# Linear attention in blocks of 64 tokens on 64x64 tiles of TensorE, and x with its tokens on partitions

## The chip, the cores and the metric

The kernel runs on one core of a Trainium2 chip. The metric is device time in microseconds (us) for one execution of the whole kernel, as the median of several executions. A matrix engine (TensorE, PE in the profile), a vector engine (VectorE, DVE), a scalar engine (ScalarE, ACT) and GpSimd (POOL) work side by side, each through its own instructions in order; SyncE (SP) issues most of the transfers. Matmul results land in eight banks of 128 partitions x 512 float32 each (PSUM), which GpSimd does not read here; everything else is in the on-chip memory SBUF.

## What is computed

Decayed linear attention over 4 batches, 8 heads, 768 tokens and a head dimension of 64, then a token mixer of rank 32, then a two-layer MLP of 512 to 2048 to 512, all in float32. Cut to what matters:

```
for b in range(nb):                      # blocks of 64 tokens, per batch and head
    intra = ((qb @ kb.T) * Dmask) @ vb   # Dmask[i, j] = lam**(i-j), lower triangle
    inter = (qb * lam**(i+1)) @ kv_state
    x[:, block] = intra + inter
    kv_state = lam**64 * kv_state + (kb * lam**(63-i)).T @ vb
u  = x + mixed                           # mixed = low-rank map over the 768 tokens
out = u + relu(u @ w_ch1) @ w_ch2
```

The block size is a matter of how the recurrence is cut, not of the result: any block size gives the same x.

## The kernel before

The work has three stages. The **front** makes x from q, k and v, mixes it over tokens, turns it and splits it for the products. The **first product** multiplies the turned u by w_ch1 (`hidden`, L624). The **second product** multiplies by w_ch2 (`product`, L760). Both products hold each float32 operand as a high and a low part, three matmuls for one.

The change lies in the front. It runs in 24 steps, one for each tile of 128 tokens of a batch (`NS` is 24, `NT`, the tiles of a batch, is 6). The instructions of every engine are issued in an order written out by hand: the list `pieces` (L494 to L508) names the pieces of each step, and L598 runs them. Side work that converts U, V and the first columns of w_ch1 from 64-bit words is dealt to the steps by `aside`.

A step s of the kernel before works on one block of 128 tokens. `prep` (L299) turns q and k of step s+1 by eight transposes on TensorE; ScalarE copies them to `qt` and `kt` (L310). `scale` (L326) lets GpSimd multiply q by powers of lam (`qs`) and k by decays (`ks`). `scores` (L334) makes k times q for each head into two banks `pss`, with keys on partitions, one head on rows 0 to 63 of the array and the other on rows 64 to 127; VectorE multiplies by the mask into `sm` (L347, two instructions). `outputs` (L350) adds the state's part (L359) and the scores' part (L364) in `px`, which has head dimensions on partitions, and ScalarE copies it to `xt` (L369). `state` (L373) makes the block's own k times v in `pkv` (L380); VectorE adds it to the faded state `kvc` (L389, four instructions), and ScalarE copies that into the block-diagonal `kv` (L395, two instructions). `back` (L399) turns `xt` so that tokens are on partitions (L404, four transposes), and ScalarE copies the result to `x_nat` (L406).

From step 7 on, three more pieces run on an earlier tile: `mix` (L444) adds the mixed part to x (one matmul, one VectorE add), `turn` (L455) turns u by four transposes and VectorE makes high and low parts (L469, L480), and the closure `rest` (L482), run as `turned` one step later, makes two ScalarE copies and one GpSimd subtraction (L486). When a batch's six tiles are complete (steps 6, 12 and 18), `low` and `low_sum` (L411, L431) compute its rank-32 part.

All PSUM tiles come from one pool with two buffers for each of the four tags a1, a2, b1 and b2. The first product starts while the last pieces of the front are still open: `rest` (L691) places them between its matmuls.

```
step += [("mix", done)] * (done >= 0)
step += [("outputs", s)]
step += [("scores", s + 1), ("back", s)] * (s + 1 < NS)
step += [("turn", done)] * (done >= 0 and done // TG < FG)
```

## Time and profile before

| what | value |
| --- | --- |
| median of 8 runs | 699.95 us (698.78 to 700.42) |
| profiled execution, its own time | 698.78 us |
| span of the profiled execution | 697.0 us |
| front, start to the first matmul of the first product | 141.6 us |
| first product | 141.6 to 420.9 us |
| second product | 420.9 to 697.0 us |
| TensorE busy in the front | 136.8 of 141.6 us |
| VectorE, ScalarE, GpSimd busy in the front | 104.6, 101.3, 66.9 us |
| busy share of the transfer engines, 0 to 50.7 and 50.7 to 141.6 us | 0.90 and 0.63 |
| granted TensorE clock | 1.00 throughout |

How to read it: the profile gives each engine's busy time, the duration of each group of instructions by source line and shape, the chain of work that ended last (followed back from the last instruction), and for every wait of an engine what ended it. A float32 matmul that is not a transpose shows as two records on PE and two weight loads on PEld; a transpose shows as one. Matmuls overlap in the pipeline, so the time from one start to the next tells more than a duration: a record of pkv lasts 222 ns, yet sixteen of them take 0.5 us. The profiled execution was the fastest of the eight; 1.8 us of its time lie around the span.

### The profile page before, as it was taken

To read this page: it belongs to the slowest core of one execution; us is meant where nothing else is said; L and a number is where in the kernel's file an instruction comes from. 1 tells how busy PE (TensorE), PEld (TensorE's weight loads), DVE (VectorE), ACT (ScalarE), POOL (GpSimd) and SP (SyncE) were. 2 spreads that over 40 slices of the span, in tenths; PEclk is the share of its full clock that TensorE was granted. 3 is DMA by queue.
4 is the path that set the end of the run, shared out by engine and by line. 5 is a ranking of instruction groups with operands and counts; after the bars stand their busy time and mean duration, and the time that the engine had idled before them with its cause. 6 is when DMAs were issued, how large, how long until landed. Compare 5 with 4: busy or idle time off the path is not lost.

```text
span 697.0 us, 11418 instructions
## 1 busy us (share of the span) xinstructions
PE 685.5 (98%) x4194; PEld 555.5 (80%) x4194; DVE 502.2 (72%) x905; ACT 306.5 (44%) x543; POOL 108.1 (16%) x91
## 2 busy tenths in 40 slices
PE   8999999998999999999999999999999999999997
PEld 6979787876888888888888888888888888888886
DVE  5778687867899777777779435777687586775864
ACT  4867777844566544444455322232232222322320
POOL 4425555523000000000000000011030030300300
PEclk9999999999999999999999999999999999999999
DMA  9977686224476565656557889966344363353531
GB/s 212 226 192 184 175 215 165 83 90 162 171 260 240 204 211 208 208 209 207 203 207 261 293 315 354 342 204 200 99 156 149 91 211 101 124 184 91 166 92 60
DMA packets 131530, 131.17 MB, mean 188 GB/s; under 512 B 81234, under 2 KB 89426, under 8 KB 131474
## 3 DMA queue, kind: packets, MB, share of 16 engines
q1 hardware_dynamic: 129376, 129.92, 59.0%
q10 hardware_dynamic: 2098, 0.52, 0.3%
q8 instruction: 33, 0.54, 0.3%
q14 instruction: 23, 0.19, 0.1%
HBM read 80.09 MB, written 50.33 MB: 187 GB/s over the span
## 4 chain that ended last, share of the span: by engine, by line
PE 93%; DVE 4%; issue 1%; ACT 1%; DMA 1%; ACTq 0%; DVEq 0%
PE pz L638 25%; PE pz L771 13%; PE pz L769 13%; PE pd L773 13%; PE pd L648 13%; PE pss L341 3%; PE px L364 3%; PE px L359 2%; PE pxn L404 2%; PE pkv L380 2%; PE put L464 1%; PE pk L306 1%; PE pq L306 1%; DVE ut L469 1%; DVE sm L347 1%
## 5 line engine op out<-in xcount | busy, mean ns | idle before, releaser
L638 PE MATMUL pz<-u_hl,w 128*128 128x512 f32 x768 | 190.7, 398 | 1.1 <-ACT uf L476 1.1
L638 PEld LDWEIGHTS pz<-u_hl,w 128*128 128x128 f32 x768 | 144.4, 188 | 37.1 <-ACT uf L476 1.5
L771 PE MATMUL pz<-w_hl,m 128*128 128x512 f32 x384 | 151.6, 396 | 0.0
L769 PE MATMUL pz<-w_hl,m 128*128 128x512 f32 x384 | 151.6, 396 | 0.0
L773 PE MATMUL pd<-w_d,m 128*128 128x512 f32 x384 | 150.0, 396 | 0.0
L752 ACT ACTIVATE m<-mt 128x512 fp32r<-128x512 f32 x96 | 60.7, 632 | 196.3 <-PE pd L773 133.3
L753 DVE SCALAR_TENSOR_TENSOR m<-rm,m 128x512 fp32r<-128x512 f32 x96 | 71.5, 745 | 49.5 <-ACT m L752 49.2
L653 DVE SCALAR_TENSOR_TENSOR r<-pd,r 128x512 f32<-128x512 f32 x96 | 61.8, 686 | 57.7 <-ACT r L644 47.2
L793 POOL TENSOR_TENSOR o<-o,u 128x512 f32<-128x512 f32 x20 | 29.9, 1523 | 452.1 <-DVE o L791 452.1
L648 PE MATMUL pd<-u_d,w 128*128 128x512 f32 x384 | 98.8, 397 | 0.0
L773 PEld LDWEIGHTS pd<-w_d,m 128*128 128x128 f32 x384 | 72.3, 188 | 17.6
L769 PEld LDWEIGHTS pz<-w_hl,m 128*128 128x128 f32 x384 | 72.3, 188 | 17.6
L771 PEld LDWEIGHTS pz<-w_hl,m 128*128 128x128 f32 x384 | 72.3, 188 | 17.6
L648 PEld LDWEIGHTS pd<-u_d,w 128*128 128x128 f32 x384 | 72.2, 188 | 17.4
L644 ACT ACTIVATE r<-pz 128x512 f32<-128x512 f32 x96 | 51.9, 592 | 62.8 <-PE pz L638 62.8
L754 DVE SCALAR_TENSOR_TENSOR m<-m 128x512 fp32r<-128x512 f32 x96 | 69.1, 721 | 0.9
L751 DVE TENSOR_SCALAR mt<-rm 128x512 uint32<-128x512 uint32 x96 | 46.2, 482 | 30.0 <-DMA rm<-r_d 29.6
L347 DVE TENSOR_TENSOR sm<-pss,mask 128x512 f32<-128x512 f32 x48 | 30.9, 686 | 10.9 <-PE pss L341 8.9
L179 ACT CAST w<-wt 128x512 fp32r<-128x512 f32 x32 | 19.9, 622 | 41.8 <-DVE wt L176 33.6
L364 PE MATMUL px<-sm,vraw 128*64 128x128 f32 x384 | 35.8, 274 | 0.4 <-DVE x_nat L450 0.3
L359 PE MATMUL px<-qs,kv 128*64 128x128 f32 x320 | 32.1, 279 | 0.0
L136 ACT ACTIVATE sc<-sc,ends 128x512 f32<-128x512 uint32 x29 | 21.0, 723 | 19.2 <-DVE sc L132 19.2
(88 smaller groups left out, 761.3 us busy)
## 6 DMA issues: line engine op xcount, KB each, us to landing
r_d<-r SPq DMA_DIRECT2D x96, 256.0 KB, 2.9
rm<-r_d SPq DMA_DIRECT2D x96, 256.0 KB, 2.7
words<-in_moe_w_ch_dram SPq DMA_DIRECT2D x32, 512.0 KB, 4.6
w_d<-w SPq DMA_DIRECT2D x16, 768.0 KB, 3.3
w_hl<-w_d SPq DMA_DIRECT2D x16, 512.0 KB, 6.6
u_d<-x_nat SPq DMA_DIRECT2D x24, 256.0 KB, 3.1
u<-u_d SPq DMA_DIRECT2D x24, 256.0 KB, 4.3
out_dram<-o SPq DMA_DIRECT2D x24, 256.0 KB, 2.0
```

What stands on the lines that cost most here:

```text
L364: nc.tensor.matmul(out=px[x * D : (x + 1) * D, a, :], lhsT=vr[:, 2 * a + x, :], rhs=sm[:, x, a, :], start=(c == 0), stop=True,)
L638: nc.tensor.matmul(out=acc[g][0], lhsT=w[:, n, ct, :], rhs=uhl[g][:, n, ct, :], start=(ct == 0 and n == 0), stop=(ct == CT - 1 and n == 1),)
L644: nc.scalar.mul(rs[g], acc[g][0], 1.0 + E)
L648: nc.tensor.matmul(out=acc[g][1], lhsT=w[:, 2, ct, :], rhs=ud[g][:, ct, :], start=(ct == 0), stop=(ct == CT - 1),)
L653: nc.vector.scalar_tensor_tensor(rs[g], acc[g][1], 4096.0, rs[g], ALU.mult, ALU.add)
L751: nc.vector.tensor_scalar(t.bitcast(U32), r.bitcast(U32), HI, None, ALU.bitwise_and)
L752: nc.scalar.activation(out=m[:, 0], in_=t, func=AF.Relu)
L753: nc.vector.scalar_tensor_tensor(m[:, 1], r, 0.0, hi, ALU.max, ALU.subtract)
L754: nc.vector.scalar_tensor_tensor(m[:, 2], hi, E, low, ALU.mult, ALU.subtract)
L769: nc.tensor.matmul(out=pz, lhsT=m[:, 0, cols], rhs=hl[:, 0], start=first, stop=False)
L771: nc.tensor.matmul(out=pz, lhsT=m[:, 1, cols], rhs=hl[:, 1], start=False, stop=end)
L773: nc.tensor.matmul(out=pd, lhsT=m[:, 2, cols], rhs=dd, start=first, stop=end)
```

## The change

The attention part of a step now takes its 128 tokens as two blocks of 64, and each of its matmuls takes 64 rows and 64 columns of the array, so that four of them have disjoint quarters of it.

- `ahead_of(s)` takes the place of `scores` and `state`. For each head and each block it multiplies `ks` with v (16 matmuls into half of a two-bank tile `psk`) and k with q (16 matmuls into the other half). VectorE then forms the state before the second block, `kvb` (one addition to the already faded state), the state after it, `kva` (four instructions), and the masked scores `sm` in one instruction instead of two. `sm` has two buffers.
- `fade(s)` is new: four ScalarE instructions that multiply `kva` by lam**64.
- `inter(s)` and `intra(s)` take the place of `outputs` and `back`. The sums have tokens on partitions, so `xt`, its four transposes and its copy are gone; one ScalarE copy takes `px` to `x_nat`.
- Because two row groups of the array add to the same sums, a small ScalarE copy `seen` waits for the last matmul of `inter`, and the second half of `intra` waits for `seen`.
- The block-diagonal `kv` and its two ScalarE copies are gone; masks and powers are 64 wide; `powers` runs before the first step; `ks` is made for every tile, the last of a batch included.
- In the front every PSUM tile has one buffer: `psk` and `px` take two banks each, and q, k, the turned u and the mixer's product take one each. The former pool is opened when the front's is closed.
- The order within a step is new: `scale` comes before `turned` on GpSimd, and `mix` of tile 17 moves from the first product to the end of the front. k and v get a fourth raw buffer, and more loads are issued at the start.

```
+    def fade(s):
+        if s % NT > 0:
+            st[s]["faded"] = faded = att.tile([P, HP, D], FP32, tag="faded", name="faded")
+            for a in range(HP):
+                nc.scalar.mul(faded[:, a, :], kva[s][:, a, :], lamc[:, a, :])
+
+    def ahead_of(s):
+        ks, vr, qt, kt = (st[s].pop("ks"), raw[s, "v"], st[s]["qt"], st[s]["kt"])
+        both = two_banks("psk", "sk")
+        c = s % NT
+        pss = both[:, :, 0 : HP * D].rearrange("p x (a i) -> p x a i", a=HP)
+        pkv = both[:, :, HP * D :].rearrange("p t (a e) -> p t a e", a=HP)
+        blocks = range(2 if c < NT - 1 else 1)
+        for a in range(HP):
+            for x in range(2):
+                for t in blocks:
+                    nc.tensor.matmul(
+                        out=pkv[half[x], t, a, :], lhsT=ks[half[t], a, x, :],
+                        rhs=vr[half[t], 2 * a + x, :], start=True, stop=True,
+                    )
+        for a in range(HP):
+            for t in range(2):
+                for x in range(2):
+                    nc.tensor.matmul(
+                        out=pss[half[t], x, a, :], lhsT=kt[half[x], a, half[t]],
+                        rhs=qt[half[x], a, half[t]], start=True, stop=True,
+                    )
+        kvb[s] = att.tile([P, HP, D], FP32, tag="kvb", bufs=2, name="kvb")
+        if c == 0:
+            nc.vector.tensor_copy(out=kvb[s], in_=pkv[:, 0])
+        else:
+            nc.vector.tensor_tensor(
+                out=kvb[s], in0=pkv[:, 0], in1=st[s].pop("faded"), op=ALU.add
+            )
+        if c < NT - 1:
+            kva[s + 1] = att.tile([P, HP, D], FP32, tag="kva", bufs=2, name="kva")
+            for a in range(HP):
+                nc.vector.scalar_tensor_tensor(
+                    kva[s + 1][:, a, :], kvb[s][:, a, :], lamc[:, a, :], pkv[:, 1, a, :],
+                    ALU.mult, ALU.add,
+                )
+        sm = att.tile([P, 2, HP, D], FP32, tag="sm", bufs=2, name="sm")
+        nc.vector.tensor_tensor(out=sm, in0=pss, in1=mask, op=ALU.mult)
+
+    def inter(s):
+        c = s % NT
+        st[s]["px"] = both = two_banks("px", "px")
+        px = both[:, :, 0 : HP * D].rearrange("p x (a e) -> p x a e", a=HP)
+        for a in range(HP):
+            for x in range(2):
+                for t, kv in enumerate((kva, kvb)):
+                    if t > 0 or c > 0:
+                        last = nc.tensor.matmul(
+                            out=px[half[t], x, a, :], lhsT=st[s]["qs"][half[x], a, t, :],
+                            rhs=kv[s][half[x], a, :], start=(a == 0), stop=False,
+                        )
+        st[s]["seen"] = nc.scalar.copy(
+            att.tile([P, 1], FP32, tag="seen", name="seen"), small[:, 4:5]
+        )
+        wait_for(st[s]["seen"], last)
+
+    def intra(s):
...
+        for i in range(2):
+            for a in range(HP):
+                for t in range(2):
+                    x = i ^ t
+                    mm = nc.tensor.matmul(
+                        out=px[half[t], x, a, :], lhsT=sm[half[t], x, a, :],
+                        rhs=vr[half[t], 2 * a + x, :],
+                        start=(c == 0 and t == 0), stop=(a == HP - 1 or (c == 0 and t == 0)),
+                    )
+                    if i == 1 and seen is not None:
+                        wait_for(mm, seen)
+                        seen = None
+        xs[s] = x_pool.tile([P, C], FP32, tag="x", name="x_nat")
+        nc.scalar.copy(xs[s].rearrange("p (a x e) -> p x a e", a=HP, x=2), px)
...
-        step = [("prep", s + 1)] * (s + 1 < NS)
-        step += [("turned", done - 1)] * (done > 0)
-        step += [("scale", s + 1)] * (s + 1 < NS)
-        step += [("aside", s)]
+        step = [("prep", s + 1), ("fade", s + 1)] * (s + 1 < NS)
         step += [("mix", done)] * (done >= 0)
         step += [("low", b - 1)] * (c == 0 and b > 0)
-        step += [("outputs", s)]
+        step += [("inter", s)]
+        step += [("scale", s + 1)] * (s + 1 < NS)
+        step += [("turned", done - 1)] * (done > 0)
+        step += [("aside", s)]
+        step += [("ahead_of", s + 1)] * (s + 1 < NS)
         step += [("low_sum", b - 1)] * (c == 0 and b > 0)
-        step += [("scores", s + 1), ("back", s)] * (s + 1 < NS)
+        step += [("intra", s)]
         step += [("turn", done)] * (done >= 0 and done // TG < FG)
         pieces += step
+    pieces += [("mix", NS - NT - 1)]
...
-        (0, 0, "mix", c0 - 1), (0, 4, "back", NS - 1), (0, 4, "enter", None),
+        (0, 4, "enter", None),
```

## The prediction

> **What bounds the kernel now.** I read the stage windows first: both products keep TensorE busy 98 to 99% and the change leaves their instructions alone, so the 141.6 us front decides. Next the chain of waits (start, length, what), here one late step of the front, from the scores of tile 16 to those of tile 17:

> ```profile
> 95.76 1.09 PE pss L341 x16
> 96.85 0.60 PE pxn L404 x4
> 97.45 0.44 PE put L464 x4
> 97.89 0.44 PE pq L306 x4
> 98.33 0.43 PE pk L306 x4
> 98.99 0.37 PE px L359 x4
> 100.89 0.55 PE pkv L380 x16
> 101.44 1.09 PE pss L341 x16
> ```

> Nothing but PE stands there; `mix` (0.24 us) lies before px at 98.99, and px runs to 100.89. Then the windows of an early step and of two late ones (bounds, length, busy PE, PEld, DVE, ACT, POOL, clock, transfer share, GB/s):

> ```profile
> 16.18:21.10 4.92, 4.92 (x79) 4.56 (x78) 3.25 (x11) 3.93 (x9) 2.34 (x2) 1.00 1.01 234
> ...
> 84.33:90.01 5.68, 5.68 (x84) 5.14 (x83) 4.63 (x10) 4.08 (x8) 3.03 (x4) 1.00 0.69 173
> ...
> 95.76:101.44 5.68, 5.68 (x83) 5.14 (x83) 4.63 (x10) 5.05 (x10) 2.44 (x3) 1.00 0.89 241
> ```

> PE fills every step; the other engines have about 1 us to spare in 5.68. So a cut on PE counts until one of them, or the transfers, binds. Steps 0 to 5 cost 4.9 us; the 15 late ones 5.7; steps 6, 12 and 18, with `low`, about 7.5.

> **TensorE, the main term.** The question is how many small matmuls run at once. One row of the groups by form (busy us, mean ns), then of PE's timeline (start, length) tell:

> ```profile
> L380 PE MATMUL pkv<-vraw,ks 128*64 128x64 f32 x49 | 2.3, 228 | 0.0
> ...
> 89.32 0.69 PE L380 MATMUL pkv<-vraw,ks 128*64 128x64 f32 x16
> 89.94 1.16 PE L341 MATMUL pss<-qt,kt 64*128 64x128 f32 x16
> ...
> 73.83 1.06 PE L415 MATMUL pp<-x_nat,u_w 128*32 128x512 f32 x8
> 74.71 0.61 PE L424 MATMUL pp<-x_nat,u_w 128*32 128x256 f32 x8
> ```

> pkv's 16 records start in pairs, one per column half, every 58 ns: 8 slots in 0.47 us. pss's start in pairs, one per row half, every 111 ns: 8 slots in 0.89, and 0.2 more of its 1.09 for the change of tiling. pp has four column quarters: 8 records take 0.88 us where one 512-wide float32 record alone takes 0.53 (pr, 1.07 for two), so four run together. The window of its start shows four records begun in 0.04 us:

> ```profile
> 73.82:73.86 0.04, 0.03 (x4) 0.03 (x5) 0.00 (x0) 1.00 0.54 205
> ```

> No row shows halves of rows and of columns at once. Its price per record of N=64 lies between 58/4 = 14.5 ns and 58 ns (no overlap). I take 14.5: halves overlap fully in either direction, quarters do in one, and records begin about 7 ns apart.

> Late step before: prep 0.87, mix 0.24, put 0.44, px 1.90, pkv 0.55, pss 1.09, pxn 0.59 = 5.68. After: prep, mix, put stay, 1.55. inter, pkv and pss have 16 matmuls each, 32 records in 8 slots of 58 ns, 0.47 each, 1.41. intra has the same 32 records, but token block and rows coincide, so only two tiles are used: 16 slots, 0.93. Changes of tiling fall from four a step to two, 0.4. Sum **4.3 us**. Early (no mix, no put): 3.6.

> [...] The rows say 128 attention records cost 2.34 us. [...]

> **VectorE.** One of two sm instructions goes (686 ns each), kvb comes (128x256, 425 ns as the copy at L387); kva's four take 0.86, as kvc's did. From 4.63 to about 4.4 busy. Laid end to end: ut 0.69, u_hl 0.62, mix 0.61, kvb 0.37, kva 0.86, sm 0.65, side work 0.6 on average, 0.2 of semaphores: **4.6**. This is the next bound.

> **ScalarE.** Gone: xt 0.58 and two kv copies of 0.405. New: four fades and `seen`. No row has an ACT instruction of 64 columns; the copies of 512 (587 ns) and 256 columns (372) put one at about 0.21, and a scaled one, as te's 631, at 0.26. Between 0.15 (overlapped) and 0.35 each; I take 0.22, 0.9 together, and 0.2 for `seen`. From a mean of 4.57 over three late steps to 4.3.

> **The added wait.** `seen` waits on ACT for inter's last matmul; behind it are u_hl's and te's copies, side casts and the copy to x_nat, and POOL's subtraction waits for te. intra's second half waits for `seen`; behind it on PE are turn and the next prep. Walk from prep's start: q is turned after 0.69 (pq at 97.89 in the chain, as ACT starts qt), qt 0.48, kt 0.6, fades 0.9, `seen` 0.3, second half of intra 0.47, put with its change 0.6: 4.05 round the loop. It is shorter than VectorE's 4.6, which hides it; uncovered, a late fade costs PE its own length. psk's single tile is free once sm has read it, some 2 us of VectorE before it is needed; px's when x_nat is copied, before inter.

> **GpSimd and queues.** qs 1.28, ks 1.06, the subtraction 1.28: 3.6 of 4.6, and with scale first qs no longer queues behind te. The extra ks (four in all) hide there. SP issues the same loads, v after intra, u's store after turn; ks(s+2) needs k two steps ahead, which the fourth buffers serve. Transfers: q, k, v are 0.786 MB a step, 3.4 us at 234 GB/s, and the early window is at share 1.01. Early steps can hardly go below 3.6; I charge **1.5 us** for the lag. Late ones need 4.2 us of transfer time (3.4, and u's 0.25 MB at some 0.35 MB/us) below 4.7.

> **Ends.** v and ks now stand before the first scores: v's load, issued at 2.29, lands after 5.5 (its row), 7.8; pss ended at 8.34 and will at about 8.8: 0.5 lost, halved masks and early `powers` fit before it. At the other end pxn (0.44) leaves the first product, but mix of tile 17 is followed by VectorE's addition (0.68 and 0.25 to be seen) before pz may reuse the bank: 0.5 lost net.

> **Sum.** Late cadence 4.7 (VectorE's 4.6, 0.1 of hand-over) for 5.68: 0.98 x 15 = 14.7. Early 3.9 for 4.9: 1.0 x 6 = 6.0. Steps with `low` lose VectorE's and ACT's slack: 0.8 x 3 = 2.4. Less 1.5, 0.5, 0.5: **20.6 us**. The profiled execution's own time is 698.8 (the lowest of eight, median 699.95, so the median may come out a microsecond higher): **678 us**.

> **Rivals.**
> - [...] 0.13.
> - *Hand-overs*: VectorE, ACT and PE all near 4.5, single PSUM buffers and `seen` make each wait for the slowest of the step, cadence 5.3 and early 4.5: 0.38 x 15 + 0.4 x 6 + 1 = 9, **689**. For: side work is uneven, 1.4 us of ACT in some steps (L136, L137). Against: two steps' slack on sm. 0.15.
> - *Tiles pair at most two at a time*, 29 ns a record: 1.95 + 3.7 = 5.65, **697 to 699**, no change. 0.05.
> - *Slower*: row and column halves don't overlap in this form, so that weight load and matmul of one tile hold the next. Place: the 128 attention records; it decides above (5.68 - 1.95) / 128 = 29 ns a record, which is pkv's present pace. At 40 ns a step is 7.1, 24 x 1.4 = 34 more, **733**. For: PEld is busy 5.14 of 5.68. Against: both directions overlap singly. 0.07.
> - That the four-wide work doesn't happen is covered by the last two.

> My case has 0.60. Its own best end is cadence 4.4 and early 3.6 (PE's), 28 to 30 us, 668. Up to the two rivals at 688 and 689 with 3 us of spread: **667 to 692**, leaving 0.12 out. A measurement tells some 0.2% (1.4 us) from no change: faster 0.88, within 0.05, slower 0.07.

> **What would show it.** Late steps (pss to pss) of 4.6 to 4.8 us with VectorE at 4.4 busy and PE idle some 0.4; inter, pkv and pss each in 0.5 to 0.65 us, intra in about 1; PE waiting for VectorE more than for ACT; the first product's first matmul near 121 us and the stages behind it as long as before. I am wrong if the 64x64 groups take 0.9 us or more, if fades exceed 0.35 us each, if PE's waits are on transfers, or if the products lengthen.

## The result, and the profile after

The changed kernel takes **695.3 us** as a median of 11 runs (692.77 to 698.51), against 699.52 us for the kernel before in the same comparisons (31 runs, 698.62 to 701.09): a ratio of 0.994, with a 95% interval from 0.9929 to 0.9952. It is faster, by some 4 us, where the prediction's sum had 20.6; 678.0 is missed by 17.3 us and the range's upper end by 3.3. The profiled execution's own time is 693.19 us around a span of 691.4.

The first product starts at 136.35 us instead of 141.61 and everything behind it is as long as before (555 us), so the whole difference lies in the front, and so does the whole miss: the forecast had about 121.

First what went as forecast. The chain of waits of the kernel after, over one late step (start, length, what):

```profile
50.16 0.62 PE px L417 x32
50.78 0.47 PE psk L379 x32
51.25 0.47 PE psk L386 x32
51.72 0.93 PE px L435 x32
52.65 0.59 PE put L504 x4
53.24 0.44 PE pq L329 x4
53.67 0.44 PE pk L329 x4
54.11 0.23 PE pu L487
54.34 0.62 PE px L417 x32
```

The step takes 4.18 us where the old one took 5.68. Thirty-two records of the state products take 0.47 us, of the scores 0.47, of `intra` 0.93, of `inter` 0.47 and the change of tiling. Four 64x64 tiles do run at once: four records of `inter` start between 50.55 and 50.57 us, and each lasts 0.22. Now windows of the kernel after: two stretches of the front, and two whole steps, one undisturbed and one near the end (bounds, length, busy PE, PEld, DVE, ACT, POOL, clock, transfer share, GB/s):

```profile
16.00:49.00 33.00, 25.92 (x798) 21.61 (x790) 19.94 (x49) 19.60 (x53) 13.42 (x12) 0.95 0.88 208
...
84.00:106.00 22.00, 15.84 (x528) 14.36 (x529) 19.41 (x36) 13.61 (x35) 13.90 (x12) 1.00 0.81 208
```

```profile
58.64:63.10 4.46, 4.46 (x146) 4.11 (x147) 4.39 (x11) 3.75 (x12) 3.74 (x3) 1.00 1.00 241
119.54:124.56 5.02, 5.02 (x201) 4.71 (x205) 4.92 (x13) 4.99 (x15) 4.78 (x4) 1.00 0.46 145
```

And the same two stretches in the kernel before:

```profile
16.00:49.00 33.00, 32.02 (x459) 27.34 (x455) 23.60 (x51) 23.84 (x47) 12.71 (x11) 1.00 0.91 214
...
84.00:106.00 22.00, 22.00 (x314) 19.86 (x312) 18.01 (x41) 17.00 (x34) 12.21 (x11) 1.00 0.79 204
```

TensorE was busy 32.0 and 22.0 us in these two stretches before; now it stands for 7.1 of 33 us and for 6.2 of 22. For what does it stand? The waits of TensorE from 7 to 136 us (line, what for, us in total, times, longest):

```profile
PE px L435 <- issue: 6.6, 5, 2.0
PE pq L329 <- issue: 3.6, 2, 2.1
PE px L417 <- issue: 1.6, 3, 1.0
PE px L417 <- ACT x_nat L444: 1.4, 1, 1.4
PE psk L379 <- DMA vraw<-in_v_dram: 1.4, 1, 1.4
PE pk L329 <- DVE vp L480: 1.2, 3, 0.7
PE pk L329 <- issue: 1.0, 1, 1.0
```

12.8 of these us (6.6, 3.6, 1.6 and 1.0) are "issue": time in which the engine waited for nothing that the profile shows. TensorE has no such wait in the front of the kernel before, where all its waits from 7 us on come to 1.4 us. One of them in the chain, ahead of the transposes of q:

```profile
86.65 0.60 PE put L504 x4
87.25 2.05 issue
89.30 0.60 PE pq L329 x4
89.90 0.44 PE pk L329 x4
```

In the records of that stop the first weight load of `pq` starts at 86.97 us, so its semaphores had been passed; the matmul that belongs to it starts at 89.30. Between this weight load and its matmul stands no wait at all, as if TensorE had not yet got the next instruction. The queue of the transfers that carry instructions fits that. Here are the rows of the list of queues, first before, then after (packets, MB, share of 16 engines):

```profile
q8 instruction: 33, 0.54, 0.3%
```

```profile
q8 instruction: 44, 0.72, 0.4%
```

Eleven more packets of 16,384 bytes, all in the front: 15 before its end in the kernel before, 26 after. TensorE issues 3,755 weight loads, matmuls and semaphore instructions there before and 6,649 after, so 250 and 256 to a packet. If the stops are TensorE running out of a packet, they must lie where packets meet. Numbering its instructions from the first one and dividing by 256 gives, for the stops of over 0.35 us between 15 and 134 us (worked out from the records; the packet is the last one that started before the restart):

```
stop (us)          length  awaited by name  remainder  packet starts  to restart
 20.03 -  21.04     1.01   nothing             193         18.82         2.22
 24.17 -  25.19     1.02   nothing             194         22.97         2.22
 28.20 -  30.23     2.03   nothing             194         27.57         2.66
 35.62 -  37.16     1.53   nothing             193         34.71         2.45
 40.43 -  40.99     0.56   nothing             194         38.68         2.31
 48.57 -  49.27     0.70   vp                  246
 83.67 -  84.11     0.44   nothing             193         81.40         2.70
 87.24 -  89.30     2.06   nothing             193         86.92         2.38
 92.87 -  93.41     0.54   nothing             194         90.61         2.80
 97.90 -  99.75     1.85   nothing             194         97.47         2.27
103.73 - 105.34     1.61   nothing             194        102.88         2.46
131.45 - 132.88     1.43   x_nat               119
```

All ten stops without a named wait restart at remainder 193 or 194, the two with one do not. So these look like the packets' boundaries. The cause, as it looked before any experiment: a step of the new kernel is some 293 records in 4.46 us (the window above), a packet's worth every 3.9 us; the old one is 166 in 5.68, a packet's worth every 8.8. In this kernel no packet's first instruction ran less than 2.19 us after the packet had started, and a packet started 1.9 us after the boundary before it (a median of 25 packets). The two add to some 4.1 us for 256 instructions, an estimate of the least time between two boundaries, and the new steps use them in just about that.

### The profile page after: what moved, and what is told of

The parts are those of the page before. It is cut to its first block, busy times and chain, and to the rows that moved or that the text cites. A ratio compares the mean times of both kernels' runs of the same rounds, so it can differ in the third digit from the quotient of the medians.

```text
span 691.4 us, 14352 instructions
## 1 busy us (share of the span) xinstructions
PE 662.6 (96%) x5634; PEld 535.7 (77%) x5634; DVE 502.8 (73%) x918; ACT 297.1 (43%) x583; POOL 117.9 (17%) x98
## 4 chain that ended last, share of the span: by engine, by line
PE 90%; DVE 5%; issue 3%; ACT 1%; DMA 1%; ACTq 0%; DVEq 0%
PE pz L685 25%; PE pz L818 13%; PE pz L816 13%; PE pd L820 13%; PE pd L695 12%; PE px L435 3%; PE px L417 2%; PE psk L379 2%; PE psk L386 2%; PE put L504 1%; PE pk L329 1%; PE pq L329 1%; DVE ut L509 1%; DMA vraw<-in_v_dram 1%; PE pp L455 1%
## 5 line engine op out<-in xcount | busy, mean ns | idle before, releaser
L695 PEld LDWEIGHTS pd<-u_d,w 128*128 128x128 f32 x384 | 72.2, 188 | 17.4
L352 POOL TENSOR_TENSOR qs<-qt,powq 128x512 f32<-128x512 f32 (+1 forms) x24 | 28.4, 1185 | 44.8 <-ACT qt L333 32.9
L435 PE MATMUL px<-vraw,sm 64*64 64x64 f32 x768 | 29.1, 220 | 6.6 <-issue 6.6
L435 PEld LDWEIGHTS px<-vraw,sm 64*64 64x64 f32 x768 | 26.2, 135 | 9.5 <-issue 9.5
L136 ACT ACTIVATE sc<-sc,ends 128x512 f32<-128x512 uint32 x29 | 21.0, 723 | 19.2 <-DVE sc L132 19.2
```

Source lines behind the costliest of these rows:

```text
L435: mm = nc.tensor.matmul(out=px[half[t], x, a, :], lhsT=sm[half[t], x, a, :], rhs=vr[half[t], 2 * a + x, :], start=(c == 0 and t == 0), sto ...
L695: nc.tensor.matmul(out=acc[g][1], lhsT=w[:, 2, ct, :], rhs=ud[g][:, ct, :], start=(ct == 0), stop=(ct == CT - 1),)
```

## The experiments

Each ratio is against the kernel before on the same chip; "stops" are TensorE's waits for "issue" from 7 us to the end of the front in the profiled execution, 12.8 us in the changed kernel.

**Loads that are shorter.** The changed kernel, with the same bytes of q, k and v read as contiguous rows of 2 KB; the tokens and heads that meet are then other ones, so x is that of permuted data.

```diff
-                in_=source[b, h : h + n, c * P : (c + 1) * P, :].rearrange("h p d -> p h d"),
+                in_=source[b].rearrange("h s d -> (h s d)")[c * P * C : (c + 1) * P * C].rearrange(
+                    "(p h d) -> p h d", h=H, d=D
+                )[:, h : h + n, :],
```

> The changed kernel, but each q, k and v load takes the same 256 KB as 128 rows of 2 KB instead of 1024 rows of 256 bytes (tokens and heads arrive permuted, so x differs from the reference); instructions of the engines are unchanged. Pages theory (TensorE stops because its own instructions arrive in 16 KB pages that land late while the transfer engines are loaded): the stops with no named wait shrink from some 12 us in the front to under 5, time 684 to 690. Data theory (TensorE waits for q, k or v and the profile doesn't name it): about the same, 683 to 690. Hand-over theory (ScalarE and VectorE in order, the seen wait): within 1 us of the changed kernel's 695.

Measured: 691.9 to 693.4 us in three executions, ratio 0.9904 (0.9887 to 0.992). A gain of some 2.5 us over the changed kernel, less than either theory of transfers expected. The fourth execution, the profiled one, took 2272 us, so no line of it tells where the gain comes from. Inconclusive.

**More instructions in the old kernel.** The kernel before, with each 128-column matmul of `pss` and `px` issued as two of 64 columns.

```diff
-            for x in range(2):
-                rows = slice(x * D, (x + 1) * D)
+            for cols in (slice(0, D), slice(D, P)):
+                for x in range(2):
...
-                    out=pss[x][:, a, :], lhsT=kt[rows, a, :], rhs=qt[rows, a, :],
+                    out=pss[x][:, a, cols], lhsT=kt[rows, a, :], rhs=qt[rows, a, cols],
```

> The kernel before, with each matmul of 128 columns in px and pss issued as two of 64: the same columns streamed and the same loads, but about 260 TensorE instructions a step for 165. Pages theory: stops of 0.5 to 2 us with no named wait appear on TensorE, each within 3 us after a 16 KB instruction packet begins; time 703 to 715. Data theory and hand-over theory: data and hand-overs are as before, so within 1.5 us of 699.5.

Measured: 721.61 us, ratio 1.0319 (1.0303 to 1.0334), and not one stop. The chain of this kernel, part of a late step:

```profile
104.14 0.23 PE px L367 x8
104.37 0.47 PE pkv L383 x16
104.84 1.93 PE pss L342 x32
106.77 0.59 PE pxn L407 x4
```

32 records of `pss` take 1.93 us, as long as 32 of full width would (1.98, an estimate: twice the 0.89 and once the 0.2 for the change of tiling of the 1.09 that 16 took before). Halving the columns did not shorten `pss`, whose matmuls still load weights of 128 columns each; it did halve the records of `px`, whose weights have 64 (eight in 0.23 us, where px took 1.90 us for 32 before). So the kernel got slower by work, its 260 or so records spread over a step of some 6.6 us, and a packet lasted some 6.4 us. By the estimate of 4.1 us above no stop is due at this pace, so as an experiment on supply it fails. What it does say: 260 records a step (293 in the changed kernel) brought no stop here, at 6.6 us a step for 4.46.

**No late loads.** The changed kernel loads q, k and v for the first three tiles only and uses them again, so its x is that of three tiles' data.

```diff
+        if s >= 3:
+            raw[s, name] = kept[s % 3, name]
+            return
```

> The changed kernel with q, k and v loaded for the first three tiles only and used again by the later ones (x differs from the reference). Pages theory and data theory: the stops go, steps run at 4.3 to 4.6 us throughout and early ones below 4, the first product begins at 113 to 121 us, time 674 to 682. Theory that the dense 64x64 stream itself outruns the pages: stops of 1 to 2 us stay even with idle transfer engines, time above 688. Hand-over theory: above 690.

Measured: 682.63 us, ratio 0.9769 (0.9749 to 0.9789); the front ends at 126.05. Both are a little behind what was expected of the two transfer theories (682 at most, 121 at most). The waits of TensorE in it:

```profile
PE px L438 <- issue: 2.7, 3, 1.1
...
PE pk L332 <- issue: 0.5, 1, 0.5
```

Stops fall from 12.8 to 3.6 us with the same 44 instruction packets, and those that remain over 0.35 us without a named wait all lie at remainder 194. (One more of 0.76 us lies there too; the profile puts it down to TensorE's own `pq` before it.) A packet now starts 1.03 us after the boundary before it (median), not 1.93. Although the changed kernel waited for loaded data only once (1.4 us, at the start), taking the loads away is worth 12.7 us (12.0 by the ratios): with the loads each packet starts 0.9 us later. Not all of the gain is stops: this version's four executions were granted 0.999 to 1.000 of the clock, the changed kernel's 0.990 to 0.998, of which more at the end.

**The columns of w_ch1 fetched later.** Two fetches of words moved from steps 5 and 15 to 12 and 19.

```diff
-        (w1_steps(1), (5, 15, 16, 17, 18, 19, 20, 21)),
-        (w1_2[:3], (15, 22, 23)),
+        (w1_steps(1), (12, 15, 16, 17, 18, 19, 20, 21)),
+        (w1_2[:3], (19, 22, 23)),
```

> The changed kernel with the fetch of the second and third columns of w_ch1 moved from steps 5 and 15 to steps 12 and 19. Pages theory: less transfer load around 38 and 91 us, some of the stops go, 1 to 5 us faster than the changed kernel. Data theory: the same sign, but only if a named or unnamed wait for q, k, v is at those places. Hand-over theory: within 1 us of 695.

Measured: 696.47 us (12 runs, 692.73 to 701.07), ratio 0.9965 (0.9947 to 0.9983), stops 10.5 us. The stops moved to other boundaries (remainder 193 or 194 still). No gain, where 1 to 5 us were expected.

**Fewer instructions, the same loads.** `qt`, `kt`, `qs`, `kvb` and `kva` in bfloat16: the scores and `inter` are one pass of TensorE each, at lower precision.

```diff
-        qt, kt = (att.tile([P, HP, P], FP32, tag=n, bufs=2, name=n) for n in ("qt", "kt"))
+        qt, kt = (att.tile([P, HP, P], BF16, tag=n, bufs=2, name=n) for n in ("qt", "kt"))
```

> The changed kernel with qt, kt, qs, kvb and kva in bfloat16, so that the scores and inter are one pass each of TensorE in place of float32's passes: some 218 TensorE instructions a step in place of some 282, the same loads, stores and order; its output is of lower precision in these two products. Theory 1 (TensorE runs out of instructions while their 16,384-byte packets queue behind the loads): a packet lasts a third longer, so most stops without a named wait go (12.65 us of the front in the changed kernel, under 5 us here) and about 32 to 38 instruction packets are fetched in the whole run; TensorE's own work falls too, by up to 0.6 us a step where it binds; 680 to 687 us. Theory 2 (it is the loads of q, k and v that TensorE waits for, unseen): loads are as they were, so the stops stay near 12 us; only the cut of TensorE's work counts where no stop hides it, 690 us or more. Theory 3 (VectorE and ScalarE bind the steps): no gain, 693 to 697.

Measured: **678.41 us**, ratio 0.9703 (0.9689 to 0.9718), 38 instruction packets, the front's end at 118.96. All of theory 1's numbers came in, the time even below them. TensorE's waits from 7 to 136 us and one window, to be held against the changed kernel's above:

```profile
PE px L418 <- ACT x_nat L445: 3.6, 3, 1.6
PE psk L380 <- issue: 3.6, 6, 1.0
PE pk L330 <- DVE vp L481: 1.8, 3, 0.8
PE psk L380 <- DMA vraw<-in_v_dram: 1.4, 1, 1.4
PE psk L380 <- DVE sm L406: 1.2, 1, 1.2
```

```profile
84.00:106.00 22.00, 20.69 (x523) 16.71 (x518) 21.62 (x49) 18.08 (x47) 17.18 (x15) 1.00 0.99 252
```

Waits for "issue" are 4.0 us in all (3.6 and 0.4, one of them not among these lines), and of these only one, of 0.40 us, lies at a packet's boundary (194). The other six, 3.6 us, are at 235, 55, 20 and such, and are of another kind: each restarts 0.10 us after VectorE has ended `sm` (worked out from the records), as the one of 1.2 us does that the profile puts down to `sm`. The state products of a next tile wait there until `sm` has read the single `psk`. The transfers move 252 GB/s here at share 0.99, where they moved 208 at 0.81 in the changed kernel: q, k and v can be delivered faster than it used them, so it was not waiting for them. Not all of the gain is supply, though. The front is 17.4 us shorter, and stops at boundaries fell by 12.4. TensorE's shorter work adds to that (`inter` 0.25 us for 0.62, the scores 0.12 for 0.47 in its chain), and new waits, 4.8 us for `sm` among them, take part of it back. The chain of a stretch in which TensorE doesn't bind:

```profile
101.58 0.32 ACT qt L334
...
102.05 0.33 ACT kt L334
...
102.53 1.08 ACT faded L367 x4
103.69 0.42 ACT u_hl L525
104.11 0.64 ACT te L526
...
105.61 0.33 ACT qt L334
```

That is ScalarE alone from one `qt` to the next in 4.03 us, four fades in it. The prediction's ring of 4.05 us went through TensorE; ScalarE's own queue is as long here, and uncovered only now.

**Loads spread out.** The changed kernel, with the load of a next k after the scores.

```diff
-        for name in "qk":
-            load_next(name)
+        load_next("q")
...
+        load_next("k")
```

> The changed kernel with the load of a next k issued at the end of the scores in place of beside that of q, so that q, k and v start in three places of a step and not in two. The same bytes, the same instructions. Theory 1 (instruction packets start late behind bursts of loads): the bursts are smaller, the stops without a named wait shrink by 1 to 4 us, 691 to 694 us. Theory 2 (transfers bind as a whole in the early steps): a k that starts later lands later, no gain or up to 2 us lost, 695 to 698. Theory 3 (VectorE and ScalarE bind): no change.

Measured: 694.84 us, ratio 0.9934 (0.9919 to 0.9949), stops 13.4 us: not to be told from the changed kernel. A packet starts 1.93 us after its boundary, as before the edit.

**The start.** Step 0's scores before its state products, and the first v second on SyncE's queue.

```diff
-        ("q", nc.sync), ("k", nc.scalar), ("v", nc.scalar), ("q", nc.sync), ("k", nc.sync)
+        ("q", nc.sync), ("k", nc.scalar), ("v", nc.sync), ("q", nc.sync), ("k", nc.sync)
...
+        for part in (products, states) if s == 0 else (states, products):
+            part()
```

> The changed kernel with step 0's scores issued before its state products, as before the change, and the first v loaded from SyncE's queue, second there. The order of the start alone: theory (the wait for v at 6.36 to 7.72 us and TensorE's half clock until 13.16 us cost what the change's start lost): the clock is full by about 9 to 10 us, the first scores start near 6.4 us, gain 1 to 2.5 us, 692.5 to 694.5 us. Rival (the front's early steps wait for transfers anyway, so the start's gain is lost by step 3): within 0.5 us of the changed kernel, 695 to 696.

Measured: 691.26 us, ratio 0.9901 (0.9876 to 0.9926): 4.0 us less than the changed kernel by medians, 2.7 by the ratios, where 1 to 2.5 were expected; stops are at 12.2. In the trace the first scores start at 6.4 us, and its records of the granted clock begin, at full, at 9.34 us, not at 13.16 (8.29 in the kernel before). What lies ahead of the first record is counted as full in the windows, but TensorE is at about half its pace there: in the changed kernel's chain the same four transposes take 1.05 us in one step and 0.59 (with a change of tiling) in the next:

```profile
2.29 5.29 DMA vraw<-in_v_dram
...
7.72 1.13 PE psk L379 x29
...
9.70 1.05 PE pq L329 x4
...
14.81 0.59 PE pq L329 x4
```

**Both of the last two.**

> The last two edits together: a next k is loaded after the scores, step 0's scores come first and the first v is second on SyncE's queue. If the two losses are apart (start and clock; instruction packets late behind bursts), the gains add to 2 to 6 us: 689 to 693 us. If the early steps wait for transfers whatever the order, 694 to 697.

Measured: 691.45 us, ratio 0.9897 (0.9856 to 0.9938), stops 11.6. So it is no better than the start's edit alone; the two gains that were expected do not add, as the other edit has none.

**bfloat16 and the start.** The edits of the two runs shown above, together.

> The changed kernel with qt, kt, qs, kvb and kva in bfloat16 (lower precision in the scores and in inter) and, of the start, step 0's scores first and the first v second on SyncE's queue. The start alone measured 4.0 us less than the changed kernel, bfloat16 alone 16.9 us less. If the two losses are apart (instructions late in the whole front; a late v and a half clock at its start): 674 to 676 us. If bfloat16's run already holds the start's gain, because transfers at share 1.00 set its early steps: 677.5 to 679.

Measured: 679.6 us (677.74 to 681.78), ratio 0.9718 (0.9695 to 0.9741): the second branch, no gain. In its first 25 us TensorE waits 2.5 us for q to land, which it does for 0.6 in the changed kernel's; so here transfers hold up the first steps. Stops at boundaries come to 2.0 us in this run, so they are not wholly gone from bfloat16.

**bfloat16 and no late loads.** The second half of the pair.

> bfloat16 qt, kt, qs, kvb, kva as before, and q, k and v loaded for the first three tiles only and used again for the others, so its output is that of three tiles' data. In float32 the loads' absence was worth 12.7 us. Theory 1 (loads cost TensorE time because they delay its instruction packets, and with fewer instructions that is mostly gone): the same edit is now worth less than half as much, 1 to 6 us, 672.5 to 677.5 us. Theory 2 (TensorE waits for the loaded data, unseen in the trace, or for the memory they share): worth as much as before, 12 to 13 us, 665 to 667. Between 667 and 672 both take part.

Measured: 678.66 us, ratio 0.9698 (0.9678 to 0.9718). The edit that was worth 12.7 us in float32 is worth nothing here by the median (1 to 6 us were expected of theory 1, 12 to 13 of theory 2); no wait for "issue" remains. Its waits for `sm` are named:

```profile
PE psk L383 <- DVE sm L409: 5.8, 8, 1.3
```

So the loads' price depended on the instructions that ran beside them. Since other engines bind the bfloat16 kernel, a small gain of TensorE could be hidden here. A hidden wait for the data of the loads is ruled out by the bfloat16 version itself: it has all loads and yet steps of 4.03 us.

**Less for GpSimd.** The changed kernel computes the scaled k of the first two tiles only and uses it again, so x is that of two tiles' scaled k.

```diff
+        if s >= 2:
+            st[s]["ks"] = kept_ks[s % 2]
+            return
```

> The changed kernel (float32), with GpSimd's scaled k computed for the first two tiles only and used again for the others, so its output is that of two tiles' scaled k. GpSimd has some 1.2 us less to do in each step; all other instructions and all loads stay. Theory (GpSimd's long operations stretch VectorE's side instructions that touch SBUF alone: 1.3 to 1.5 us for lines 132, 133, 145, 153 and 187 where the kernel before has 0.42 to 0.68): most of these come back to 0.42 to 0.75, and the stretch in which VectorE sets the end (119 to 136 us) gives up 1 to 2.5 us: 692 to 694.5 us. Rival (they are stretched by transfers or by ScalarE): durations and time stay, 695 to 696.

Measured: 692.62 us, ratio 0.991 (0.9884 to 0.9935), a gain of 2.7 us by medians; the intervals of the two ratios overlap by a little, so it isn't clear of noise. Its profiled execution was its longest run, with 14.4 us of stops. Three of the five lines named in the expectation came back: L187 to 681 ns on average from 20 us on (1402 in the changed kernel), L133 to 398 (1106) and L153 to 566 (757). L132 and L145 did not.

**Less for GpSimd, in bfloat16.**

> The bfloat16 version (678.4 us) with the scaled k of the first two tiles used again for all others. There VectorE is busy 21.6 of 22 us in the late steps, some 7 us of side instructions stretched among them. If VectorE's stretched side work sets its steps: 2 to 4 us less, 674.5 to 676.5 us. If ScalarE's chain does (qt, kt, four fades, seen, te: 4.1 us a step in the chain from 98 to 108 us): under 1 us, 677.5 to 678.5.

Measured: 674.08 us, ratio 0.9638 (0.9622 to 0.9654): 4.3 us less than the bfloat16 version, but only 2.0 of that lie in the front, which ends at 116.96 for 118.96. The rest lies behind it, in 555.0 us for 557.4: the bfloat16 version ran at a granted clock of 0.50 across the front's end (the window below), and this one was granted a mean of 0.999 over its span.

```profile
117.49:124.32 6.83, 6.04 (x18) 3.94 (x22) 2.56 (x6) 1.41 (x3) 1.73 (x2) 0.50 0.21 77
```

In the front VectorE's L188 (L187 above) came back from 1244 to 682 ns on average and L134 (L133 above) from 1155 to 400. So the 2.0 us fit the theory that VectorE's stretched side work counts, at the low end of its 2 to 4; that the lighter load of GpSimd itself gave some of them isn't excluded. How the work is stretched can be seen at the end of the changed kernel's front; the timelines of VectorE and of GpSimd (start, length; in brackets, idle time before and what ended it):

```profile
125.15 1.50 DVE L187 SCALAR_TENSOR_TENSOR w<-wt,wf 128x512 fp32r<-128x512 f32 x1
126.58 0.41 DVE L394 TENSOR_TENSOR kvb<-psk,faded 128x256 f32<-128x256 f32 x1
...
130.32 0.43 DVE L132 TENSOR_SCALAR sc<-words 128x512 uint32<-128x512 uint32 x1
130.65 1.51 DVE L133 TENSOR_SCALAR m<-words 128x512 uint32<-128x512 uint32 x1
```

```profile
125.05 1.06 POOL L341 TENSOR_TENSOR ks<-kraw,small 128x512 f32<-128x512 f32 x1
126.39 1.41 POOL L526 TENSOR_TENSOR u_d<-te,u_hl 128x512 fp32r<-128x512 f32 x1 [0.28 <-ACT te L525]
...
130.58 1.30 POOL L526 TENSOR_TENSOR u_d<-te,u_hl 128x512 fp32r<-128x512 f32 x1 [1.30 <-ACT te L525]
```

With no operation of GpSimd beside them, in the kernel before, L187 took 0.68 us (at 87.98) and L133 0.42 (at 135.32). In the rows above each started within 0.1 us after a GpSimd operation of 1.06 or 1.30 us and took 0.8 and 1.1 us more, a little less than what was left of that operation (0.96 and 1.23). `kvb`, which reads PSUM, kept its length beside GpSimd's `u_d`: 0.41 us, where the median of its twenty is 0.418. The kernel before has one such row too: L133 took 1.52 us at 45.68, beside a `qs` of 1.39 us that GpSimd had begun at 45.52. By what mechanism the work is stretched isn't shown.

## Why the prediction was wrong in size

**The step that failed** is the term "Late cadence 4.7 (VectorE's 4.6, 0.1 of hand-over) for 5.68", and its early counterpart of 3.9. Both summed what each engine executes and whom it waits for by semaphore. No term stood for TensorE's own instructions, which the change nearly doubles (83 matmul records in a late step before, about 146 after) and makes short. They come by transfer, 256 to a packet by the counts above, and the profile counts the packets' time on the 16 engines that the loads of q, k and v keep busy (a share of 0.88 from 16 to 49 us). Charged for transfers were 1.5 us of lag; the stops were 12.8. The profile of before had shown the instruction queue at 0.3% of the transfers; the packets' bytes are negligible, and their lateness isn't. The prediction named "PE's waits are on transfers" as a sign of being wrong; it came, but for transfers that it had not counted, and without a name in the profile.

That it is supply is shown: by the stops' place at every 256th instruction, in the changed kernel and in six float32 versions of it, whose stops fall at different times; by the weight load parted from its matmul; by the packet's start ahead of each restart; by the fall of the stops to 3.6 us without the loads and, at boundaries, to 0.4 with fewer instructions (2.0 in the two later versions of that kind that kept the loads). The two terms of a packet, worked out from the records of the front (us; the first packet left out of the medians):

```
kernel            boundary to next packet's start   packet's start to its first
                  median                            instruction, smallest
before            0.31                              6.02
after             1.93                              2.19
no late loads     1.03                              2.24
loads spread      1.93                              2.22
the start         1.80                              2.26
bfloat16          1.62                              2.25
bfloat16, no
 late loads       0.75                              2.96
```

Before, every packet started at least 6 us before it was needed. After, the smallest lead is 2.19 to 2.26 us in the four float32 versions, whatever the loads and their order; the loads change the first term, 1.93 us with them and 1.03 without the late ones. Whether they do so by standing ahead of the packet in the transfer engines or in some other way isn't shown. Nor are they the whole of it: the kernel before has the same loads and a median of 0.31, and why its packets start sooner is open.

Without the stops the front would end near 124 us (an estimate, 136.35 less 12.8). The trace has none at 166 records in 5.68 us, and 12.8 us of them where a step is 293 records in 4.46 beside full transfers (a share of 1.00).

The other steps, in the prediction's order:

- **TensorE, 4.3 us a late step.** Right: 4.18 to 4.46 from 50 to 67 us, with 14.7 ns a record (0.47 us for 32). The rival at 688, which also stands behind the range's upper end, rests on a least price of a record that no run shows; the runs showed these 14.7 ns in its place. The rival of two tiles at a time has fallen. That its time, 697 to 699, comes nearest is luck: the gain was there and was lost elsewhere.
- **VectorE, 4.6, the next bound.** Right at the front's end, where it is busy 16.8 of 17 us and steps take 5.0 to 5.2. The sum lacked the stretch of side instructions: L187 1.50 us for 0.68, L133 1.51 for 0.42.
- **ScalarE's fades at 0.22, 0.9 for four.** Too low: 343 ns each and 1.08 us for four, at the upper bound of 0.35. No wait of TensorE shows it here; in the bfloat16 kernel they are part of a stretch that ScalarE sets.
- **The added wait, `seen`.** Right: the list of waits has none for it that matters.
- **GpSimd and queues.** "SP issues the same loads" is true, and GpSimd kept up; what the loads share the transfer engines with was left out.
- **Ends.** v landed at 7.58 as forecast (7.8). The 0.5 us charged was too small: the start's repair is worth 4.0 us by medians, 2.7 by the ratios. The first scores ended at 9.70, not 8.8, as TensorE ran at about half its pace (four transposes in 1.05 us for 0.59) until about 13.16 us, where the records of its clock begin (8.29 before). How much of the loss is v's wait and how much that pace isn't separated.
- **Hand-overs as a rival (689).** Not the cause: of TensorE's waits in the front, ScalarE and VectorE end 1.7 and 2.5 us, at a few places.
- **A slip that decides nothing.** In the third window ScalarE had 0.6 us to spare, not about 1.

The miss adds up roughly: stops of 12.8 us for the 1.5 charged are 11.3, the start 2.7 to 4.0 for 0.5 is 2.2 to 3.5, and a stretch of 3.41 us at half the clock behind one stop (last section) costs at most 1.7. Together that is 15.2 to 16.5, and the profiled execution missed 678.0 by 15.2. The remaining 2.1 us of the median's 17.3 lie between that execution and the median. One candidate is the clock: the profiled execution was granted 0.998 of the clock and the others 0.990 to 0.995 (0.999 to 1.000 in the kernel before). Over 691 us that is 3.5 to 6.9 us of clock lost for 1.4, an estimate and an upper bound. But the times don't follow the clock one by one (0.990 took 695.49 us, 0.993 took 698.51), so this is not shown. The changed kernel varies by 0.8% from run to run where the old one varies by 0.35%; stops that depend on when each packet starts, and half clocks behind some of them, would explain it, but that too is argued.

The fastest version that computes the whole result is the bfloat16 one, 678.41 us, at lower precision in two products; in float32 it is the one with the start repaired, 691.26.

## What to carry to other kernels

When a change cuts matmuls into smaller ones, count instructions per microsecond as well as array time: here 256 of them in 8.8 us were supplied, each packet starting 6 us or more ahead of its use; 256 in some 4 us beside full transfers were not. In the profile, look for "issue" ahead of an instruction that waits for nobody, and number the engine's instructions: stops that recur at one remainder by 256 (193 or 194) were supply here. A wait for "issue" at other remainders was something else: hold its end against the ends of the other engines' work. Fewer passes all but cured it (0.4 us of stops at boundaries, 2.0 in two later versions, for 12.8); dealing the loads out differently did not (13.4). And look at the granted clock on both sides of the place that was changed before a difference is put down to the change.

## What had not been expected of the hardware

```profile
30.23:33.64 3.41, 3.41 (x47) 2.96 (x49) 1.12 (x3) 2.07 (x5) 1.03 (x1) 0.50 0.83 209
```

- In the old kernel with split matmuls, a matmul of `pss` with 64 columns on half the rows cost as much as one of 128 columns, with weights of 128 columns in both: 32 of them took 1.93 us, 54 ns each without 0.2 us for the change of tiling (an estimate), where 16 of 128 columns took 0.89 without it, 56 ns each.
- An instruction packet's own transfer took a median of 0.97 us in the changed kernel (0.92 to 1.5 at the stops), but its first instruction never ran less than 2.19 us after the transfer's start, and 2.24 without the late loads.
